# Tap weights on eight partitions and first rows of x through another queue, at the start of a convolution and feed-forward kernel

## The chip, the cores and the metric

The kernel runs on one core of one Trainium2 chip. The metric is the device time of one execution in microseconds (us). Seven kinds of work go on side by side: TensorE (PE in the profile, with its weight loads as PEld), VectorE (DVE), ScalarE (ACT), GpSimd (POOL), SyncE (SP), and the DMA engines, 16 of them, that move data for the queues of SP, ACT and POOL.

## The reference

A causal convolution of seven taps, whose weights are a softmax of a small table of 8 heads x 7 taps, and a feed-forward part on its result, with the product of two projections between:

```python
w = softmax(weight, axis=-1)                    # [8, 7]
x_pad = concat([zeros(B, 6, D), x], axis=1)     # x is [8, 3904, 192]
out[b, s, h] = sum_k w[h, k] * x_pad[b, s + k, h]   # 24 channels a head
t = out.reshape(B * S, D)                       # 31232 tokens of 192
result = (((t @ w1) * (t @ w2)) @ w3) @ w_out   # w1, w2: 192 x 1024
```

## The kernel before

**Two streams.** The 31232 tokens are cut in two halves (r = 0, 1, NS = 2), of 15616 each, and 64 partitions (Q) belong to each half. The 192 channels are three blocks of 64 (NP). So a transposed tile xT[k] holds 64 channels of both halves, and every weight tile wd[i] (i = 0 for w1, 1 for w2) is held twice: once in partitions 0 to 63 and once in 64 to 127.

**The convolution as a matmul.** A window has 64 rows of x, on the partitions, and gives 58 rows of result (ST = 64 - 6). For each head a band matrix of 64 x 64 holds the seven taps on its diagonals (Aband). It is built at the start: `band` (L252) multiplies shifted views of a diagonal (diag) by the taps on DVE into cprod (L254), and 28 small matmuls for each of four pairs of heads add them up in PSUM (L263). `conv` (L381) then multiplies windows of x (the tiles xb) by these bands (L398). Windows come in batches: batch 0 has six windows per half of the tokens, batch 1 four. The first window of each sequence has only 58 rows of x behind six rows of zeros, which is why batch 0's window 0 is loaded apart.

**The first product.** For each stretch of 512 tokens (a round R) and each 128 columns of w1 and w2, `first_factor` (L478) runs 12 matmuls (L486) into PSUM, ACT casts the one factor (L494) and DVE multiplies it by the other (L505) into abT. `second_product` multiplies abT by w3 @ w_out, which is worked out once. Rounds go in groups of four. The convolutions of later batches are put in between; their results go through DRAM (rows) and come back transposed (xT<-rows, L468).

**The order of the work** on each engine is written by hand: each engine runs its instructions in the order of the program text, and semaphores are added where data passes from one to another. The four pairs of PSUM banks (`banks`, `drained`) are handed round in that order too. A DMA is issued by an engine's queue in the same order as its other instructions.

**The start**, which the change touches:

- ACT's queue loads the table `weight` into wall, one partition of 56 values (L144). Then ACT loads its table of functions (L164).
- DVE clears some tiles (L157 to L163), among them window 0 of batch 0 of xb.
- SP's queue loads the first quarter of the columns of w1 and w2 as fp32 into wfirst (L171), 64 partitions.
- POOL's queue, which also casts to bf16 as it moves, loads batch 0 of x (L179, two loads), makes the two diagonals (L183), loads window 0's 58 rows of each half (L189, two loads), batch 1 (L126), and then the other quarters of the weights (L176) and further batches (L126). Between them POOL casts one half of wfirst into wd (`cast_w`, L193) and copies weights from the lower to the upper partitions (`copy_w`, L197).
- TensorE runs six matmuls on zeros (`warm`, L213), which give nothing and only occupy it.
- The softmax: greatest value, subtraction (DVE, L223, L224), exponential (ACT, L226), sum, reciprocal, product (DVE, L228 to L230), all on one partition. Two matmuls with a row of zeros and ones (half) spread the result to 128 partitions (L237), DVE copies it (L239), and two more matmuls on zeros follow.
- Then the four bands (`put` moves them, L584), three weight casts on ACT, the two halves of batch 0's convolution (moved by `move_all`, whose copies stand in `move`, L581), three transposes on TensorE (L456), batch 1's convolution, and the first parts of the first product.

Of the kernel before, what the change touches and what calls it, by code (L numbers as in the profile page):

```python
# [16 lines left out]
def kernel(  # L17
# [10 lines left out]
    nc = tc.nc  # L28

    B, S, D = x.shape  # L30
    H, K = weight.shape
# [3 lines left out]
    PAD = K - 1  # L35

    NS = 2
    TS = B * S // NS
# [4 lines left out]
    Q = 64  # L43
    ST = Q - PAD
# [22 lines left out]
    const = ctx.enter_context(tc.tile_pool(name="const", bufs=1))  # L67
# [10 lines left out]
    def banks():  # L78
        p = free.pop(0)
        return p, pairs[:, NS * p:NS * p + NS, :]  # L80
# [4 lines left out]
    def drained(p):  # L85
        assert p not in free
        free.append(p)
# [17 lines left out]
    x_rows = x.rearrange("b s d -> (b s) d")  # L105
    xb_of, zero_rows = {}, {}

    def x_spans(r, i, m):
        return bass.AP(tensor=x.tensor, offset=(r * TS + tok(i) - PAD) * D,
                       ap=[[D, Q], [ST * D, m], [1, D]])  # L110
# [29 lines left out]
            else:  # L140
                tiles.append((xb, 0))

    wall = const.tile([1, H, K], FP32)
    nc.scalar.dma_start(out=wall, in_=weight.rearrange("(o h) k -> o h k", o=1))  # L144

    n0 = SIZES[0] // 2
    xb0 = work.tile([128, 2 * n0, D], BF16, tag="xb", bufs=5, name="xb")
    xb_of[0] = [(xb0, 0), (xb0, n0)]
    wfirst = work.tile([Q, 2, NP, DFF // 4], FP32, tag="abT", bufs=GROUP, name="wfirst")
# [1 line left out]
    tiny = const.tile([128, 1], FP32)  # L151
    ones = const.tile([128, 1], BF16)
    zeros = const.tile([128, 128], BF16)
    half = const.tile([1, 3 * Q], BF16)
    ident = const.tile([128, 128], BF16)
    diag = const.tile([128, Q + PAD], BF16)
    nc.vector.memset(zeros, 0.0)  # L157
    nc.vector.memset(tiny, 0.0)
    nc.vector.memset(ones, 1.0)
    nc.vector.memset(xb0[:, 0, :], 0.0)  # L160
    nc.vector.memset(half, 0.0)
    nc.vector.memset(half[:, Q:2 * Q], 1.0)
    nc.vector.memset(ident, 0.0)  # L163
    nc.scalar.activation(out=tiny, in_=tiny, func=ACT.Exp)  # L164

    WC = (0, DFF // 4, DFF // 2, DFF * 3 // 4, DFF)
    wd = [const.tile([128, NP, DFF], BF16, name=f"wd{i}", tag=f"wd{i}") for i in range(2)]
    w_rows = [w.rearrange("(k q) f -> q k f", q=Q) for w in (moe_w1, moe_w2)]

    for i in range(2):  # L170
        nc.sync.dma_start(out=wfirst[:, i], in_=w_rows[i][:, :, 0:WC[1]])  # L171

    def load_w(part):
        cs = slice(WC[part], WC[part + 1])
        for i in range(2):
            nc.gpsimd.dma_start(out=wd[i][0:Q, :, cs], in_=w_rows[i][:, :, cs])  # L176

    def load_x0(r):
        nc.gpsimd.dma_start(out=xb0[Q * r:Q * r + Q, 1:, :], in_=x_spans(r, 1, 2 * n0 - 1))  # L179

    load_x0(0)
    for p0 in (0, Q):
        nc.gpsimd.affine_select(  # L183
            out=diag[p0:p0 + Q], in_=ones[p0:p0 + Q].to_broadcast([Q, Q + PAD]),
            pattern=[[-1, Q + PAD]], compare_op=ALU.is_equal, fill=0.0, base=0,
            channel_multiplier=1)
    load_x0(1)
    for r in range(NS):
        nc.gpsimd.dma_start(out=xb0[Q * r + PAD:Q * r + Q, 0, :],  # L189
                            in_=x_rows[r * TS:r * TS + ST, :])  # L190
    load_x(1)
    def cast_w(i, r, f):
        f(out=wd[i][Q * r:Q * r + Q, :, 0:WC[1]], in_=wfirst[:, i])  # L193

    def copy_w(part, i, f):
        cs = slice(WC[part], WC[part + 1])
        f(out=wd[i][Q:128, :, cs], in_=wd[i][0:Q, :, cs])  # L197

    load_w(1)
    cast_w(1, 1, nc.gpsimd.tensor_copy)  # L200
    load_w(2)
    load_x(2)
    for i in range(2):
# [6 lines left out]
    def warm(n):  # L210
        p, t = banks()
        for j in range(n):
            nc.tensor.matmul(t[:, j % 2, :], zeros, zeros[:, 0:1].to_broadcast([128, CH]),  # L213
                             start=True, stop=True)
        drained(p)

    warm(6)

    wmax = const.tile([1, H], FP32)
    wsum = const.tile([1, H], FP32)  # L220
    wrow = const.tile([1, H, K], BF16)
    wsb = const.tile([128, 2, 2, K], BF16)
    nc.vector.reduce_max(out=wmax, in_=wall, axis=AX.X)  # L223
    nc.vector.tensor_tensor(  # L224
        out=wall, in0=wall, in1=wmax.unsqueeze(2).to_broadcast([1, H, K]), op=ALU.subtract)
    nc.scalar.activation(out=wall, in_=wall, func=ACT.Exp)  # L226
    nc.vector.tensor_copy(out=ident[0:Q, 0:Q], in_=diag[0:Q, 0:Q])
    nc.vector.reduce_sum(out=wsum, in_=wall, axis=AX.X)  # L228
    nc.vector.reciprocal(out=wsum, in_=wsum)
    nc.vector.tensor_tensor(  # L230
        out=wrow, in0=wall, in1=wsum.unsqueeze(2).to_broadcast([1, H, K]), op=ALU.mult)
    nc.vector.tensor_copy(out=ident[Q:128, Q:128], in_=diag[Q:128, 0:Q])
    pw, wbc = banks()
    wbc = wbc[:, 0, 0:H * K // 2].rearrange("p (g e k) -> p g e k", g=2, e=2)
    wrow = wrow.rearrange("p (g e a) k -> p g e a k", g=2, a=2)
    for a in range(2):
        nc.tensor.matmul(wbc, half[:, Q - Q * a:Q - Q * a + 128], wrow[:, :, :, a],  # L237
                         start=(a == 0), stop=(a == 1))
    nc.vector.tensor_copy(out=wsb, in_=wbc)  # L239
    drained(pw)  # L240
    warm(2)

# [2 lines left out]
    def band_of(h, r):  # L245
        return Aband[Q * r:Q * r + Q, h // 4, (h % 4) // 2, int(h % 2 != r), :]
# [126 lines left out]
    def segments(c0, n):  # L373
        out = []
        while n:
            m = min(n, Q - c0 % Q)
            out.append((c0 // Q, c0 % Q, m))
            c0, n = c0 + m, n - m
        return out

    def conv(b, h0, nh, evict=None):  # L381
        n = SIZES[b] // 2
        if h0 == 0:
            tag, bufs = ("alone", 1) if GRID <= b else ("convo", 2)
            convo_of[b] = work.tile([128, n, NP, NS, Q], BF16, tag=tag, bufs=bufs, name="convo")
        convo = convo_of[b]
        p, cps = banks()
        wd = nh * G

        def view(ps, r):  # L390
            return cps[ps, r, 0:n * wd].rearrange("p (w g) -> p w g", g=wd)

        for j in range(nh):
            h = h0 + j
            for c in range(2):
                xb, w0 = xb_of[b][c]
                for r in range(NS):
                    nc.tensor.matmul(  # L398
                        view(slice(Q * c, Q * c + Q), r)[:, :, j * G:(j + 1) * G],
                        band_of(h, r),  # L400
                        xb[Q * r:Q * r + Q, w0:w0 + n, h * G:(h + 1) * G],
                        start=True, stop=True)
        src = cps[:, :, 0:n * wd].rearrange("p r (w g) -> p r w g", g=wd)
        o, moves = 0, []
        for k, c0, m in segments(h0 * G, wd):
            moves.append((convo[:, :, k, :, c0:c0 + m].rearrange("p w r g -> p r w g"),
                          src[:, :, :, o:o + m]))
            o += m
        if h0 + nh == H:
            del xb_of[b]  # L410
        if evict == ():
            return p, moves
        if evict == "streams":
            assert nh == H
# [163 lines left out]
    V, A, P = nc.vector.tensor_copy, nc.scalar.copy, nc.gpsimd.tensor_copy  # L578

    def move(f, pair):  # L580
        f(out=pair[0], in_=pair[1])  # L581

    def put(f, p, dst, src):
        f(out=dst, in_=src)  # L584
        drained(p)

    cast_w(0, 0, A)
    put(A, *band(0, 0))
    put(A, *band(0, 1))
    cast_w(0, 1, A)  # L590
    made = [band(1, 0), band(1, 1)]
    put(V, *made[0])
    put(V, *made[1])
    cast_w(1, 0, A)

    def move_all(p, moves, fs):
        for f, m in zip(fs, moves):
            move(f, m)
        drained(p)
# [26 lines left out]

    move_all(*conv(0, 0, 4, ()), (V, V))
    move_all(*conv(0, 4, 4, ()), (A, A))
    for k, f in enumerate((V, V, A)):
        p, *m = pe_transpose(0, k)  # L630
        move(f, m)
        drained(p)
# [51 lines left out]
    def put_rows(b, last):  # L684
# [7 lines left out]
        out=wv, in0=wv, in1=top.unsqueeze(2).to_broadcast([128, H, K]), op=ALU.subtract)  # L692
# [5 lines left out]
        out=wv, in0=wv, in1=top.unsqueeze(2).to_broadcast([128, H, K]), op=ALU.mult)  # L698
# [84 lines left out]
```

## Time and profile before

| | us |
|---|---|
| median of three runs | 517.26 |
| the three runs | 515.74, 517.26, 519.17 |
| the profiled execution | 516.65 |
| its span | 514.9 |

The span runs from the first to the last instruction in the profile; 1.75 us of the profiled execution lie around it. PEclk, the granted clock of TensorE, is 0.999 in this execution. In the profile's rows, the first number is the start in us from the beginning of the span, the second the time taken; then come the engine, the line, the operation and, after the tiles' names, how many instructions of its kind were merged in the row. In brackets stands for how long the engine had been idle before, and what ended that. ACTq, SPq and POOLq are the issuing of DMAs and the like. The chain of waits is followed back from the last instruction, each piece to what released it.

### The profile page before, as it was taken

The page shows a single profiled execution, that of the slowest core. Times are in us where ns is not written, and L with a number is a line of the kernel's source. Part 1 is how long each engine was busy: PE and PEld are TensorE (multiplying, and loading weights), DVE is VectorE, ACT ScalarE, POOL GpSimd, SP SyncE. Part 2 cuts the span into 40 slices and gives each one's busy share as a digit, 9 for nine tenths or more (in the row PEclk, how much of TensorE's full clock was granted, in tenths as well). Part 3 has the DMA queues.
Part 4 walks back from the last instruction along what each step waited for, and adds up shares of the span by engine and source line. Part 5 has one row for each costly group of instructions (what it writes and reads, how often), then busy time and mean ns, then how long its engine had stood idle before and what let it go on. Part 6 is the DMA issues. An engine that isn't in the chain of part 4 may idle for free.

```text
span 514.9 us, 13645 instructions
## 1 busy us (share of the span) xinstructions
PE 508.2 (99%) x5608; PEld 339.2 (66%) x5608; DVE 403.4 (78%) x481; ACT 350.7 (68%) x466; POOL 321.8 (63%) x447
## 2 busy tenths in 40 slices
PE   8999999999999999999999999999999999999997
PEld 4544698555894448945489454885449844598577
DVE  6788723899958999599994999949999499972970
ACT  6877645777657776577765777657776577744762
POOL 8501624289999999799984999749997491000000
PEclk9999999999999999999999999999999999999999
DMA  9998999992974983797827798288842861035004
GB/s 116 164 154 135 141 191 210 239 182 58 179 206 144 141 103 89 226 154 110 99 91 241 139 107 97 93 244 140 102 48 93 256 114 32 1 101 172 7 3 155
DMA packets 137410, 67.91 MB, mean 132 GB/s; under 512 B 98899, under 2 KB 135939, under 8 KB 137283
## 3 DMA queue, kind: packets, MB, share of 16 engines
q0 software_dynamic: 48096, 26.92, 36.6%
q1 hardware_dynamic: 89105, 40.01, 33.3%
q8 instruction: 44, 0.72, 0.6%
q14 instruction: 19, 0.16, 0.1%
q10 hardware_dynamic: 146, 0.10, 0.1%
HBM read 39.60 MB, written 36.56 MB: 148 GB/s over the span
## 4 chain that ended last, share of the span: by engine, by line
PE 95%; DMA 2%; DVE 1%; ACT 1%; POOL 1%; issue 0%; ACTq 0%
PE pairs L486 61%; PE pairs L537 31%; PE pairs L398 2%; DMA xT<-rows 1%; PE pairs L572 1%; DVE abT L505 1%; DMA xb<-in_x_dram 1%; PE pairs L611 1%; ACT asb L494 1%; DMA wall<-in_weight_dram 0%; POOL xb L189 0%; POOL xb L179 0%; POOL xb L126 0%; POOL diag L183 0%; DVE xT L624 0%
## 5 line engine op out<-in xcount | busy, mean ns | idle before, releaser
L505 DVE TENSOR_TENSOR abT<-asb,pairs 128x1024 bf16<-128x1024 bf16 (+1 forms) x245 | 297.8, 1217 | 67.4 <-ACT asb L494 51.1
L486 PE MATMUL pairs<-xT,wd 64*128 64x512 bf16 (+3 forms) x3000 | 320.0, 371 | 1.1 <-DVE abT L505 0.4
L494 ACT CAST asb<-pairs 128x1024 bf16<-128x1024 f32 (+1 forms) x245 | 247.1, 1009 | 68.7 <-PE pairs L486 68.5
L486 PEld LDWEIGHTS <-wd 64*128 64x128 bf16 x3000 | 160.8, 94 | 154.6 <-issue 3.8
L537 PE MATMUL pairs<-W_sb,abT 128*128 128x192 bf16 x1952 | 165.0, 246 | 0.0
L537 PEld LDWEIGHTS <-abT 128*128 128x128 bf16 x1952 | 159.9, 98 | 5.3 <-issue 5.1
L542 ACT COPY osb<-pairs 128x384 f32<-128x384 f32 x122 | 58.7, 481 | 83.3 <-PE pairs L537 82.5
L331 POOL TENSOR_TENSOR acc<-acc,term 128x384 f32<-128x384 f32 (+1 forms) x120 | 107.5, 896 | 9.4
L328 POOL TENSOR_TENSOR term<-xv,wv 128x384 f32<-128x384 bf16 (+1 forms) x144 | 107.9, 749 | 0.1
L317 DVE SCALAR_TENSOR_TENSOR pairs<-xv,wv,pairs 128x384 f32<-128x384 bf16 (+1 forms) x120 | 68.7, 572 | 7.2 <-ACT pairs L315 3.4
L364 POOL DMA_DIRECT2D rows<-y x6 | 3.7, 614 | 69.9 <-DVE y L320 61.1
L334 POOL TENSOR_TENSOR y<-acc,term 128x192 bf16<-128x192 f32 (+5 forms) x60 | 26.6, 470 | 1.9
L325 POOL TENSOR_TENSOR acc<-xv,wv 128x384 f32<-128x384 bf16 (+1 forms) x24 | 18.3, 764 | 10.3 <-DMA xv<-in_x_dram 10.2
L424 ACT CAST convo<-pairs 128x864 bf16<-128x864 f32 (+9 forms) x43 | 23.8, 627 | 0.1
L424 DVE CAST convo<-pairs 128x960 bf16<-128x960 f32 (+4 forms) x10 | 8.2, 857 | 17.2 <-PE pairs L398 17.2
L320 DVE SCALAR_TENSOR_TENSOR y<-xv,wv,pairs 128x192 bf16<-128x192 bf16 (+5 forms) x60 | 18.0, 351 | 1.1
L126 POOL DMA_DIRECT2D xb<-in_x_dram x20 | 13.9, 714 | 3.8 <-DMA xb<-in_x_dram 2.5
L549 POOL DMA_DIRECT2D out_dram<-osb x8 | 6.1, 764 | 14.7 <-ACT osb L542 12.0
L342 POOL DMA_DIRECT2D xb<-in_x_dram x20 | 15.1, 772 | 0.0
L447 POOL DMA_DIRECT2D rows<-convo x2 | 1.1, 544 | 20.7 <-DVE convo L420 20.7
L279 POOL DMA_DIRECT2D xv<-in_x_dram x12 | 13.0, 1086 | 0.0
L315 ACT ACTIVATE pairs<-xv,wv 128x384 f32<-128x384 bf16 (+1 forms) x24 | 12.8, 549 | 0.0
(67 smaller groups left out, 89.6 us busy)
## 6 DMA issues: line engine op xcount, KB each, us to landing
out_dram<-osb SPq DMA_DIRECT2D x52, 384.0 KB
xv<-in_x_dram POOLq DMA_DIRECT2D x10, 672.0 KB, 9.7
xb<-in_x_dram POOLq DMA_DIRECT2D x20, 216.0 KB, 7.4
rows<-y POOLq DMA_DIRECT2D x5, 768.0 KB, 5.0
out_dram<-osb POOLq DMA_DIRECT2D x8, 384.0 KB, 5.1
w3rows<-in_moe_w_dram POOLq DMA_DIRECT2D x2, 1024.0 KB, 11.2
xb<-in_x_dram POOLq DMA_DIRECT2D x8, 240.0 KB, 7.8
rows<-convo SPq DMA_DIRECT2D x6, 288.0 KB
```

What stands on the lines that cost most here:

```text
L317: f.scalar_tensor_tensor(out=flat, in0=xs(k), scalar=tap(k), in1=flat, op0=ALU.mult, op1=ALU.add)
L320: f.scalar_tensor_tensor(out=dst, in0=xv[:, 0:W, r, h * G + cs.start:h * G + cs.stop], scalar=tap(0), in1=by_row[:, :, r, cs], op0=ALU.mul ...
L325: f.tensor_tensor(out=flat, in0=xs(PAD), in1=wide(PAD), op=ALU.mult)
L328: f.tensor_tensor(out=term.rearrange("p (m g) -> p m g", g=G), in0=xs(k), in1=wide(k), op=ALU.mult)
L331: f.tensor_tensor(out=acc, in0=acc, in1=term, op=ALU.add)
L334: f.tensor_tensor(out=dst, in0=by_row[:, :, r, cs], in1=term[:, :, r, cs], op=ALU.add)
L424: f[e % len(f)](out=dst, in_=part)
L486: nc.tensor.matmul(p[:, r, e * n:e * n + n], wd[i][rs, k, ft * 128:(ft + 1) * 128], xT[k][rs, r0 + c0:r0 + c1], start=(k == 0), stop=(k == ...
L494: nc.scalar.copy(out=asb, in_=pa)
L505: nc.vector.tensor_tensor(out=dst, in0=asb, in1=pb, op=ALU.mult)
L537: nc.tensor.matmul(ops[:, (g - g0) * D:(g - g0) * D + D], ab[:, jt, r, g * 128:(g + 1) * 128], W_sb[:, jt, :], start=(jt == 0), stop=(jt = ...
L542: f(out=osb[:, g0:g0 + per, :].rearrange("p g d -> p (g d)"), in_=ops[:, 0:per * D])
```

## The change

- `weight` is loaded by SP's queue into eight partitions, seven values each (wall is [8, 7]).
- The softmax runs on eight partitions. The greatest value is taken with its sign turned and goes into the exponential as a bias, so the subtraction is gone. One instruction divides by the sum and puts each head's row on a diagonal of blocks (wrow is [8, 8, 7]).
- One matmul with ones on eight partitions spreads all 56 values to 128 partitions, and two copies of 64 partitions each take the heads that each half needs. There are five matmuls on zeros ahead of it instead of six.
- The two copies of the identity move from DVE to ACT.
- Window 0's 58 rows of each half are loaded as fp32 by SP's queue into a tile of their own (xfirst, cleared by DVE), ahead of wfirst, and ACT casts the whole tile into xb. POOL's queue no longer loads them; its second diagonal comes after the second load of batch 0.
- POOL casts the upper halves of both w1 and w2. ACT casts the lower halves in four pieces of 128 columns, of which three stand after the first two bands and the last after the convolution of batch 0.

```diff
-    wall = const.tile([1, H, K], FP32)
-    nc.scalar.dma_start(out=wall, in_=weight.rearrange("(o h) k -> o h k", o=1))
+    wall = const.tile([H, K], FP32)
+    nc.sync.dma_start(out=wall, in_=weight)
...
-    nc.vector.memset(xb0[:, 0, :], 0.0)
-    nc.vector.memset(half, 0.0)
-    nc.vector.memset(half[:, Q:2 * Q], 1.0)
+    nc.vector.memset(xfirst, 0.0)
+    nc.vector.memset(ones_h, 1.0)
...
+    for r in range(NS):
+        nc.sync.dma_start(out=xfirst[Q * r + PAD:Q * r + Q, :],
+                          in_=x_rows[r * TS:r * TS + ST, :])
     for i in range(2):
         nc.sync.dma_start(out=wfirst[:, i], in_=w_rows[i][:, :, 0:WC[1]])
...
     load_x0(0)
-    for p0 in (0, Q):
-        nc.gpsimd.affine_select(
...
+    diagonal(0)
     load_x0(1)
-    for r in range(NS):
-        nc.gpsimd.dma_start(out=xb0[Q * r + PAD:Q * r + Q, 0, :],
-                            in_=x_rows[r * TS:r * TS + ST, :])
+    diagonal(Q)
     load_x(1)
-    def cast_w(i, r, f):
-        f(out=wd[i][Q * r:Q * r + Q, :, 0:WC[1]], in_=wfirst[:, i])
+    def cast_w(i, r, f, c0=0, c1=WC[1]):
+        f(out=wd[i][Q * r:Q * r + Q, :, c0:c1], in_=wfirst[:, i, :, c0:c1])
...
     load_w(1)
-    cast_w(1, 1, nc.gpsimd.tensor_copy)
+    for i in range(2):
+        cast_w(i, 1, nc.gpsimd.tensor_copy)
     load_w(2)
...
-    warm(6)
+    warm(5)
...
-    nc.vector.reduce_max(out=wmax, in_=wall, axis=AX.X)
-    nc.vector.tensor_tensor(
-        out=wall, in0=wall, in1=wmax.unsqueeze(2).to_broadcast([1, H, K]), op=ALU.subtract)
-    nc.scalar.activation(out=wall, in_=wall, func=ACT.Exp)
-    nc.vector.tensor_copy(out=ident[0:Q, 0:Q], in_=diag[0:Q, 0:Q])
+    nc.vector.tensor_reduce(out=wmax, in_=wall, axis=AX.X, op=ALU.max, negate=True)
+    nc.scalar.activation(out=wall, in_=wall, func=ACT.Exp, bias=wmax)
+    nc.scalar.copy(out=ident[0:Q, 0:Q], in_=diag[0:Q, 0:Q])
     nc.vector.reduce_sum(out=wsum, in_=wall, axis=AX.X)
     nc.vector.reciprocal(out=wsum, in_=wsum)
-    nc.vector.tensor_tensor(
-        out=wrow, in0=wall, in1=wsum.unsqueeze(2).to_broadcast([1, H, K]), op=ALU.mult)
-    nc.vector.tensor_copy(out=ident[Q:128, Q:128], in_=diag[Q:128, 0:Q])
+    nc.vector.scalar_tensor_tensor(
+        out=wrow, in0=wall.unsqueeze(1).to_broadcast([H, H, K]), scalar=wsum,
+        in1=diag[0:H, 0:H].unsqueeze(2).to_broadcast([H, H, K]), op0=ALU.mult, op1=ALU.mult)
+    nc.scalar.copy(out=ident[Q:128, Q:128], in_=diag[Q:128, 0:Q])
+    nc.scalar.copy(out=xb0[:, 0, :], in_=xfirst)
...
+    nc.tensor.matmul(wbc, ones_h, wrow, start=True, stop=True)
     for a in range(2):
-        nc.tensor.matmul(wbc, half[:, Q - Q * a:Q - Q * a + 128], wrow[:, :, :, a],
-                         start=(a == 0), stop=(a == 1))
-    nc.vector.tensor_copy(out=wsb, in_=wbc)
+        nc.vector.tensor_copy(out=wsb[Q * a:Q * a + Q], in_=wbc[Q * a:Q * a + Q, :, :, a])
...
-    cast_w(0, 0, A)
     put(A, *band(0, 0))
     put(A, *band(0, 1))
-    cast_w(0, 1, A)
+    for i in range(2):
+        cast_w(i, 0, A, 0, 128)
+    cast_w(0, 0, A, 128)
     made = [band(1, 0), band(1, 1)]
     put(V, *made[0])
     put(V, *made[1])
-    cast_w(1, 0, A)
...
     move_all(*conv(0, 4, 4, ()), (A, A))
+    cast_w(1, 0, A, 128)
```

More of the change, by code (lines that the diff above doesn't have):

```diff
@@ L153 @@
     zeros = const.tile([128, 128], BF16)
-    half = const.tile([1, 3 * Q], BF16)
+    ones_h = const.tile([H, 128], BF16)
+    xfirst = const.tile([128, D], FP32)
     ident = const.tile([128, 128], BF16)
@@ L179, in load_x0, with diagonal @@
         nc.gpsimd.dma_start(out=xb0[Q * r:Q * r + Q, 1:, :], in_=x_spans(r, 1, 2 * n0 - 1))
-    load_x0(0)
-    for p0 in (0, Q):
+    def diagonal(p0):
         nc.gpsimd.affine_select(
@@ L186 @@
             channel_multiplier=1)
+    load_x0(0)
+    diagonal(0)
     load_x0(1)
-    for r in range(NS):
-        nc.gpsimd.dma_start(out=xb0[Q * r + PAD:Q * r + Q, 0, :],
-                            in_=x_rows[r * TS:r * TS + ST, :])
+    diagonal(Q)
     load_x(1)
-    def cast_w(i, r, f):
-        f(out=wd[i][Q * r:Q * r + Q, :, 0:WC[1]], in_=wfirst[:, i])
+    def cast_w(i, r, f, c0=0, c1=WC[1]):
+        f(out=wd[i][Q * r:Q * r + Q, :, c0:c1], in_=wfirst[:, i, :, c0:c1])
     def copy_w(part, i, f):
@@ L215, in warm @@
         drained(p)
-    warm(6)
-    wmax = const.tile([1, H], FP32)
-    wsum = const.tile([1, H], FP32)
-    wrow = const.tile([1, H, K], BF16)
+    warm(5)
+    wmax = const.tile([H, 1], FP32)
+    wsum = const.tile([H, 1], FP32)
+    wrow = const.tile([H, H, K], BF16)
     wsb = const.tile([128, 2, 2, K], BF16)
-    nc.vector.reduce_max(out=wmax, in_=wall, axis=AX.X)
-    nc.vector.tensor_tensor(
-        out=wall, in0=wall, in1=wmax.unsqueeze(2).to_broadcast([1, H, K]), op=ALU.subtract)
-    nc.scalar.activation(out=wall, in_=wall, func=ACT.Exp)
-    nc.vector.tensor_copy(out=ident[0:Q, 0:Q], in_=diag[0:Q, 0:Q])
+    nc.vector.tensor_reduce(out=wmax, in_=wall, axis=AX.X, op=ALU.max, negate=True)
+    nc.scalar.activation(out=wall, in_=wall, func=ACT.Exp, bias=wmax)
+    nc.scalar.copy(out=ident[0:Q, 0:Q], in_=diag[0:Q, 0:Q])
     nc.vector.reduce_sum(out=wsum, in_=wall, axis=AX.X)
     nc.vector.reciprocal(out=wsum, in_=wsum)
-    nc.vector.tensor_tensor(
-        out=wrow, in0=wall, in1=wsum.unsqueeze(2).to_broadcast([1, H, K]), op=ALU.mult)
-    nc.vector.tensor_copy(out=ident[Q:128, Q:128], in_=diag[Q:128, 0:Q])
+    nc.vector.scalar_tensor_tensor(
[3 more added lines that the diff above has]
+    nc.scalar.copy(out=xb0[:, 0, :], in_=xfirst)
     pw, wbc = banks()
-    wbc = wbc[:, 0, 0:H * K // 2].rearrange("p (g e k) -> p g e k", g=2, e=2)
-    wrow = wrow.rearrange("p (g e a) k -> p g e a k", g=2, a=2)
+    wbc = wbc[:, 0, 0:H * K].rearrange("p (g e a k) -> p g e a k", g=2, e=2, a=2)
+    nc.tensor.matmul(wbc, ones_h, wrow, start=True, stop=True)
     for a in range(2):
-        nc.tensor.matmul(wbc, half[:, Q - Q * a:Q - Q * a + 128], wrow[:, :, :, a],
-                         start=(a == 0), stop=(a == 1))
-    nc.vector.tensor_copy(out=wsb, in_=wbc)
+        nc.vector.tensor_copy(out=wsb[Q * a:Q * a + Q], in_=wbc[Q * a:Q * a + Q, :, :, a])
     drained(pw)
```

## The prediction

> **What bounds the kernel now.** I read the page first, then the chain of waits, then the stretches, then the first 15 us instruction by instruction.
>
> ```profile
> span 514.9 us, 13645 instructions
> ...
> PE 508.2 (99%) x5608; PEld 339.2 (66%) x5608; DVE 403.4 (78%) x481; ACT 350.7 (68%) x466; POOL 321.8 (63%) x447
> ...
> PE 95%; DMA 2%; DVE 1%; ACT 1%; POOL 1%; issue 0%; ACTq 0%
> ```
>
> TensorE carries 95% of the chain. Whether a few tenths at the start reach the end depends on idle time later. In the stretches (us, then PE's busy time) there is almost none:
>
> ```profile
> 60.00:90.00 30.00, 29.84 (x416) 27.63 (x415) 10.13 (x16) 13.89 (x32) 10.26 (x14) 1.00 1.14 198
> 90.00:515.00 425.00, 421.57 (x4444) 281.98 (x4443) 344.43 (x393) 291.85 (x372) 284.19 (x387) 1.00 0.64 126
> ```
>
> So a shift of the first product (L486) moves the end by about the same amount, and everything that the change touches lies before it. The chain of waits there:
>
> ```profile
> 0.81 1.21 DMA wall<-in_weight_dram
> ...
> 3.53 1.10 POOL xb L189 x2
> 4.63 0.59 POOL xb L126
> 5.22 4.19 DMA xb<-in_x_dram
> ...
> 9.45 0.43 PE pairs L398 x31
> 9.89 0.57 PE pairs L486 x6
> ```
>
> The last wait before the first product is the load of batch 1 of x, landing at 9.41. It was queued on POOL behind the two L189 loads. The mark to beat is the start of L486 in the timeline:
>
> ```profile
> 9.82 1.06 PE L486 MATMUL pairs<-xT,wd 64*128 64x348 bf16 x12
> ```
>
> **The softmax on eight partitions.**
>
> ```profile
> 0.81 0.52 ACTq L144 DMA_DIRECT2D wall<-in_weight_dram  x1
> 1.37 1.28 ACT L164 ACT_TABLE_LOAD   x1 [1.37 <-PEq L767]
> 2.05 0.20 DVE L223 TENSOR_REDUCE wmax<-wall 1x8 f32<-1x56 f32 x1 [0.57 <-DMA wall<-in_weight_dram]
> 2.28 0.33 DVE L224 TENSOR_TENSOR wall<-wall,wmax 1x56 f32<-1x56 f32 x1
> 2.77 0.23 ACT L226 ACTIVATE wall<-wall 1x56 f32<-1x56 f32 x1
> 4.23 2.23 DVE L254 TENSOR_TENSOR cprod<-diag,wsb 128x448 bf16<-128x448 bf16 x4
> ```
>
> The subtraction (0.33) goes into the exponential's bias; the table load no longer follows a DMA issue (0.52), so the exponential is not held by it. One copy out of PSUM becomes two, about +0.15 with overlap. The eight-partition load replaces one piece of 224 bytes by eight of 28; I take the same 1.21 (none in the trace is like it; +-0.3). Sum: L254 starts about 0.4 earlier, 3.85. Warm-up loses one of six matmuls, which stand in front of the spreading matmul and end earlier than it. The identity copies move from DVE to ACT and wait there for POOL's two diagonals; nothing else is ready on ACT then, and the second diagonal comes only 0.72 (one POOL load) later. Gain so far 0.4, if nothing else is late.
>
> **The first stretches of x.** POOL loses 1.10 of issue, so batch 1 could land at 8.3 instead of 9.41. In exchange SP issues wall and two loads of 58 rows x 768 bytes ahead of wfirst, and ACT must cast them before its next work. Here is the change's risk:
>
> ```profile
> 0.82 1.40 SPq L171 DMA_DIRECT2D wfirst<-in_moe_w_dram  x2
> 4.68 0.83 ACT L193 CAST wd<-wfirst 64x768 bf16<-64x768 f32 x1 [1.68 <-DMA wfirst<-in_moe_w_dram]
> ```
>
> wfirst's two issues took 0.70 each, starting at 0.82. With three issues of about 0.5 (the 0.52 of L144) ahead, they start near 2.3. How do 58 rows travel? The nearest row is a store on the same queue with rows of the same 768 bytes: 38 rows, L359. Its issue, and the DMA engines (40 slices of 277.45 to 277.70, tenths of 16 engines) when the earlier stores had drained:
>
> ```profile
> 275.37 1.31 SPq L359 DMA_DIRECT2D rows<-convo  x1
> ```
> ```profile
> DMA  0400003000003000030007300003000070000303
> ...
> q1 hardware_dynamic: 13, 0.01, 11.2%
> ```
>
> 11.2% of 16 is 1.8 engines: single packets, one after the other, on two engines. 13 packets in 0.25 us on two engines are 38 ns each. [...] I take it that each xfirst load puts 29 packets on the same two engines, 58 in all, and that wfirst's share there (192 rows over 16 engines, 12 per load) queues behind: 82. [...]
>
> The speed depends on what else these engines carry. The queues in the stretch 4 to 5 us, with POOL's loads running:
>
> ```profile
> q1 hardware_dynamic: 167, 0.16, 67.3%
> q0 software_dynamic: 162, 0.06, 51.0%
> ```
>
> 167 packets over 16 engines in 1 us: an engine gave SP's queue one per 96 ns, half of its 49 ns slots. After the change POOL's loads run from about 3 us as before, so I take 96, with 38 (alone) as the low end and 122 (two slots in five, an estimate) as the high one. The first packets of this queue came about 1.3 after its first issue:
>
> ```profile
> q1 hardware_dynamic: 9, 0.01, 10.1%
> ```
>
> (that is the stretch 2.0 to 2.5; only wall's lay before). xfirst is issued from about 1.35, so packets run from 2.6. xfirst: 2.6 + 58 x 0.096 = 8.2. wfirst: 2.6 + 82 x 0.096 = 10.5; the 0.4 us before POOL's loads start go faster (-0.6), the last receipt adds some 0.5: 10.4.
>
> **Who waits.** ACT works in order. The rows:
>
> ```profile
> 5.54 0.27 ACT L584 CAST Aband<-pairs 128x128 bf16<-128x128 f32 x1
> ...
> 6.28 1.69 ACT L193 CAST wd<-wfirst 64x768 bf16<-64x768 f32 x2
> ...
> 7.00 0.59 PE L398 MATMUL pairs<-xb,Aband 64*64 64x72 bf16 x32
> ...
> 7.18 0.82 POOL L193 CAST wd<-wfirst 64x768 bf16<-64x768 f32 x1
> ...
> 7.87 0.69 ACT L581 CAST convo<-pairs 128x192 bf16<-128x192 f32 x2
> ...
> 9.02 0.45 ACT L581 COPY xT<-pairs 128x348 bf16<-128x348 bf16 x1 [0.46 <-PE pairs L456]
> ```
>
> Behind ACT's cast of xfirst stand the two copies of Aband, then the weight casts, the eviction of the first convolution, the last weight cast, the copy of xT. From 768 elements at 0.83 and 128 at 0.27, an element costs 0.875 ns: the cast of 192 takes 0.33, a half weight cast of 384 takes 0.49. xfirst at 8.2 gives Aband at 8.2 + 0.33 + 0.54 = 9.1 and the first convolution (7.00 before) at about 9.1. Then ACT waits for the second wfirst load, 10.4: cast of wd1 0.49, rest of wd0 0.49, eviction 0.69, rest of wd1 0.49, xT 0.45 = 2.61, so the first product starts at 13.0. Against 9.82 that is +3.2. The gain of 0.4 in the softmax and of 1.1 for batch 1 lie under this wait and are worth nothing. At 38 ns wfirst is there at 2.6 + 3.1 + 0.5 = 6.2 and ACT is not held; at 122 ns it comes at 12.5 and the loss is 5.3.
>
> POOL casts both halves now (one more, 0.82, for the 1.10 saved) and waits for the same load: 10.4 to 12.0. Behind it stand two weight loads, batch 2 of x, and the copies of L197, which in before started when their load had landed:
>
> ```profile
> 2.81 0.72 POOL L179 DMA_DIRECT2D xb<-in_x_dram  x1
> ...
> 7.95 1.26 POOL L176 DMA_DIRECT2D wd<-in_moe_w_dram  x2
> 9.21 1.40 POOL L126 DMA_DIRECT2D xb<-in_x_dram  x2
> 10.80 1.59 POOL L197 COPY wd<-wd 64x768 bf16<-64x768 bf16 x2 [0.20 <-DMA wd<-in_moe_w_dram]
> ```
>
> ```profile
> 12.55 4.91 PE L486 MATMUL pairs<-xT,wd 64*128 64x164 bf16 x60 [0.24 <-DVE xT L624]
> ```
>
> In before POOL's casts ended at 8.0 and the copies at 12.4; the columns that they fill are first read after the 24 matmuls of 164 columns that head the last row, near 13.3: 0.9 to spare. Now the casts end at 12.0, the loads behind them take 1.26 and 1.40 of issue, and the copies end near 16.3, while TensorE comes to these columns at 13.3 + 3.2 = 16.5. Nothing is added, but the cover is thin: 0.5 more on POOL would cost 0.3.
>
> **The sum.** 516.65 (the profiled execution: span 514.9 and 1.75 around it) + 3.2 = 519.8. The median of the runs shown, 517.26, stands 0.6 above that execution, and its runs spread from 515.74 to 519.17; I keep the sum.
>
> **Rivals.** *It is quick enough* (faster than before). The two loads share their engines at the 38 ns end, or are spread wider. For it: they start before POOL's traffic. Then the Aband copies end near 5.9, three half casts bring ACT to 7.4, eviction 8.1, cast 8.6, xT 9.05; the first product starts near 9.4, 0.4 early, up to 0.9 if ACT's order yields more. 516.2. It decides if wfirst has landed by about 7.0, that is 50 ns per packet; against it stands the 96.
>
> *TensorE falls back to its slow start.* The row of warm-up matmuls and one from later:
>
> ```profile
> 1.07 2.74 PE L213 MATMUL pairs<-zeros 128*128 128x512 bf16 x6 [1.07 <-DVE ones L159]
> ```
> ```profile
> 68.11 2.75 PE pairs L537 x32
> ```
>
> 0.457 us for 512 columns first, later 0.086 for 192, that is 0.229 for 512: half speed at first, although the granted clock reads 1.00 in all stretches. With two pauses of 2 to 3 us each in the start, the first parts could run at half speed again; another 3.4 us or so of that costs 1.7 at most: 521.5. [...]
>
> *POOL's queue crowds SP's out* (122 ns): +5.3, 522.0.
>
> **How the numbers follow.** Main case 0.55 (its own range 518.2 to 521.0), quick 0.28 (515.7 to 516.6), slow start 0.10, crowded 0.07. Leaving out about a tenth at each end gives 515.8 to 521.4. This kernel's measurement tells about 1% (5.2 us) from no change: faster by that 0.01, slower (above 521.8, most of the crowded case and a tail of the slow start) 0.08, within 0.91.
>
> **What would show it.** In the changed profile: the cast of xfirst on ACT should idle until about 8 on its DMA, the cast of wd1 until about 10.4, and the first L486 product start near 13.0; a stretch of the DMA with few engines on SP's queue should be seen late. If ACT's Aband copies start before 6 and the first product before 9.5, the two-engine price was wrong. If the first product is 3 late but the end is not, later slack swallowed it, and the reading of the stretches was wrong.

## The result, and the profile after

The changed kernel is slower by 0.41%: 518.8 us in the median of 22 runs (517.8 to 520.47) against 516.74 (515.57 to 520.62, 22 runs). The ratio is 1.0041, with a 95% interval from 1.0028 to 1.0053, that is 1.4 to 2.7 us, 2.1 in the middle. The forecast was 519.8, 3.2 above the execution that it started from.

The page of the changed kernel, whose profiled execution took 517.8, its fastest (that of before, 516.65, lay near the middle of its own):

```profile
span 516.1 us, 13646 instructions
...
PE 509.3 (99%) x5606; PEld 338.6 (66%) x5606; DVE 402.9 (78%) x478; ACT 350.8 (68%) x470; POOL 321.1 (62%) x446
...
PE 97%; DMA 1%; DVE 1%; ACT 0%; issue 0%; POOL 0%; POOLq 0%; ACTq 0%; DVEq 0%
```

The shares hardly differ; the start does. From its timeline (line numbers after the change are two to three higher):

```profile
0.82 0.40 SPq L144 DMA_DIRECT2D wall<-in_weight_dram  x1
1.28 0.60 SPq L171 DMA_DIRECT2D xfirst<-in_x_dram  x2
1.92 1.36 SPq L174 DMA_DIRECT2D wfirst<-in_moe_w_dram  x2
...
4.17 2.23 DVE L256 TENSOR_TENSOR cprod<-diag,wsb 128x448 bf16<-128x448 bf16 x4
...
5.33 0.35 ACT L236 CAST xb<-xfirst 128x192 bf16<-128x192 f32 x1 [1.55 <-DMA xfirst<-in_x_dram]
...
6.81 0.24 PE L400 MATMUL pairs<-xb,Aband 64*64 64x72 bf16 x1
6.85 0.51 ACT L196 CAST wd<-wfirst 64x384 bf16<-64x384 f32 x1 [0.56 <-DMA wfirst<-in_moe_w_dram]
...
7.91 0.92 ACT L196 CAST wd<-wfirst 64x384 bf16<-64x384 f32 x2 [0.55 <-DMA wfirst<-in_moe_w_dram]
...
8.13 0.69 PE L400 MATMUL pairs<-xb,Aband 64*64 64x72 bf16 x31 [1.08 <-DMA xb<-in_x_dram]
...
10.95 1.92 PE L488 MATMUL pairs<-xT,wd 64*128 64x348 bf16 x12
```

Three things are to be seen. The rows of window 0 were cast at 5.33 and the last of wfirst was there at 7.91, much earlier than the forecast's 8.2 and 10.4. The wait that decided is on another transfer: the first convolution begins at 6.81, where it began at 7.00 before, stops after one matmul and goes on at 8.13, when a load of xb lands. And the first product then starts at 10.95 (9.82 before) and its first 12 matmuls take 1.92 (1.06 before). The chain of waits names the transfer, and shows what is left at the middle of the kernel:

```profile
2.46 5.63 DMA xb<-in_x_dram
...
61.08 5.39 PE pairs L574 x64
```

It is the second load of batch 0 by POOL's queue (issued at 2.46), landing at 8.09. The same load landed 3.9 after an issue at 2.81 before, at 6.7. And the matmuls themselves, grouped by shape (the two numbers behind the bar are the busy time in us and the mean ns of one), in the first 16 us, before and then after:

```profile
L486 PE MATMUL pairs<-xT,wd 64*128 64x348 bf16 x24 | 2.1, 309 | 0.0
L456 PE MATMUL pairs<-ident,convo 128*128 128x128 bf16 x9 | 0.8, 219 | 0.6 <-DVE convo L581 0.5
```
```profile
L488 PE MATMUL pairs<-xT,wd 64*128 64x348 bf16 x24 | 3.0, 399 | 0.0
L458 PE MATMUL pairs<-ident,convo 128*128 128x128 bf16 x9 | 1.2, 306 | 0.5 <-DVE convo L583 0.5
```

The same instructions run longer. So the loss has two parts: +1.13 at the first product (10.95 - 9.82), and +0.61 from there to the products for W_sb: these start at 61.08, and in the chain of before at

```profile
59.34 5.39 PE pairs L572 x64
```

which makes +1.74. Later the kernel before loses some of this lead: in it the transposed rows of the next round came late (4 matmuls at 89.16, the rest from 89.92), and after the change they did not (from 90.89 on without a pause). That leaves +1.40, which stays to the last copy (511.65 and 513.05); the spans end 1.2 apart. In the medians it is 2.1; one profiled execution cannot say which part grows in the others.

### The profile page after: what moved, and what is told of

Its sections match the earlier page's. It is cut to its first block, busy times and chain, and to the rows that moved or that the text cites. A ratio compares the mean times of both kernels' runs of the same rounds, so it can differ in the third digit from the quotient of the medians.

```text
span 516.1 us, 13646 instructions
## 1 busy us (share of the span) xinstructions
PE 509.3 (99%) x5606; PEld 338.6 (66%) x5606; DVE 402.9 (78%) x478; ACT 350.8 (68%) x470; POOL 321.1 (62%) x446
## 4 chain that ended last, share of the span: by engine, by line
PE 97%; DMA 1%; DVE 1%; ACT 0%; issue 0%; POOL 0%; POOLq 0%; ACTq 0%; DVEq 0%
PE pairs L488 61%; PE pairs L539 32%; PE pairs L400 2%; DMA xb<-in_x_dram 1%; PE pairs L574 1%; DVE abT L507 1%; PE pairs L613 1%; ACT asb L496 0%; PE pairs L458 0%; POOL xb L182 0%; DVE convo L583 0%; ACT osb L544 0%; POOL diag L185 0%; POOLq L185 0%; ACTq L544 0%
## 5 line engine op out<-in xcount | busy, mean ns | idle before, releaser
L126 POOL DMA_DIRECT2D xb<-in_x_dram x20 | 13.9, 714 | 3.9 <-DMA xb<-in_x_dram 2.7
L551 POOL DMA_DIRECT2D out_dram<-osb x8 | 6.1, 763 | 13.9 <-ACT osb L544 10.9
L400 PE MATMUL pairs<-xb,Aband 64*64 64x216 bf16 (+6 forms) x416 | 12.7, 245 | 1.1 <-DMA xb<-in_x_dram 1.1
```

Source lines behind the costliest of these rows:

```text
L400: nc.tensor.matmul(view(slice(Q * c, Q * c + Q), r)[:, :, j * G:(j + 1) * G], band_of(h, r), xb[Q * r:Q * r + Q, w0:w0 + n, h * G:(h + 1) ...
```

## The experiments

All ratios are to the kernel before, with 95% intervals. First the parts, alone and left out, and the way of the rows on SP's queue.

**x_only**: before, with the rows of window 0 alone taken over.

```diff
+    for r in range(NS):
+        nc.sync.dma_start(out=xfirst[Q * r + PAD:Q * r + Q, :], in_=x_rows[...])
     for i in range(2):
         nc.sync.dma_start(out=wfirst[:, i], ...)
...
-    for r in range(NS):
-        nc.gpsimd.dma_start(out=xb0[Q * r + PAD:Q * r + Q, 0, :], ...)
...
+    nc.scalar.copy(out=xb0[:, 0, :], in_=xfirst)
     cast_w(0, 0, A)
     put(A, *band(0, 0))
```

> The kernel before with one part of the change: window 0's rows as fp32 on SP's queue ahead of wfirst, ScalarE's cast of them ahead of its first weight cast; softmax, spreading and weight casts as before. If the rows' way is the cause (either reading of it), the second load of batch 0 lands near 8, the first product starts at 10.7 or later and the time is 1.2 to 2.5 us above before. If the loss came from the softmax or the regrouped casts, the first product starts at 9.8 +- 0.3 and the time is within 0.6 of before.

1.0059 (1.0046 to 1.0071): this part alone costs what the whole change costs, or more, 3.0 us where 1.2 to 2.5 were expected. Here ACT's whole weight cast stands ahead of the copies of Aband and waits for wfirst:

```profile
6.95 0.83 ACT L194 CAST wd<-wfirst 64x768 bf16<-64x768 f32 x1 [1.31 <-DMA wfirst<-in_moe_w_dram]
...
7.99 0.67 PE L399 MATMUL pairs<-xb,Aband 64*64 64x72 bf16 x32 [0.90 <-ACT Aband L585]
```

The first product started at 11.44. The cause of the convolution's wait is not the one expected; the place is.

**no_x**: the changed kernel, rows of window 0 back on POOL's queue.

```diff
-    for r in range(NS):
-        nc.sync.dma_start(out=xfirst[...], ...)
...
     diagonal(Q)
+    for r in range(NS):
+        nc.gpsimd.dma_start(out=xb0[Q * r + PAD:Q * r + Q, 0, :], ...)
     load_x(1)
...
-    nc.scalar.copy(out=xb0[:, 0, :], in_=xfirst)
```

> The changed kernel with window 0's rows back on POOL's queue, casting on the way; softmax and weight casts as changed. If the rows' way is the cause, the first convolution starts at 6.9 to 7.1, the first product at 9.4 to 9.8 and the time is 0 to 0.6 us below before. If the softmax or the casts are to blame, the first product stays after 10.5 and the time 1.5 or more above before.

1.0050 (1.0035 to 1.0065), so the theory fell in the form that it had: without the rows on SP's queue the loss stays. The convolution waited for x again, this time for window 0's rows on POOL's queue (issued at 3.46, the first of them landing at 7.61),

```profile
7.75 0.76 PE L398 MATMUL pairs<-xb,Aband 64*64 64x72 bf16 x32 [0.69 <-DMA xb<-in_x_dram]
```

and the first product came at 10.64. Each part alone is enough, and together they don't add up: the first convolution waits in all three kernels, but each time something else comes last, ACT's copies of Aband behind wfirst (x_only), window 0's rows (no_x) or batch 0's second load (the change).

**split** and **w_ahead**: the changed kernel with each load of 58 rows cut in two, and with wfirst's loads ahead of them.

```diff
     for r in range(NS):
-        nc.sync.dma_start(out=xfirst[Q * r + PAD:Q * r + Q, :], ...)
+        for s0, s1 in ((0, 48), (48, ST)):
+            nc.sync.dma_start(out=xfirst[Q * r + PAD + s0:Q * r + PAD + s1, :], ...)
```

> The changed kernel, each load of 58 rows cut into 48 and 10 rows. Two-engine reading: spread over more engines, the rows no longer hold two engines up, the second load of batch 0 lands by 7.2, the first product starts by 10.0 and the time is within 0.7 us of before. Order reading (wfirst, issued 1.1 us later, now runs against batch 0's loads): two more issues push wfirst a further 0.5 back, the load lands at 8 or later, the first product starts at 10.9 or later and the time stays 2 us above before.

```diff
-    for r in range(NS): ... xfirst
     for i in range(2): ... wfirst
+    for r in range(NS): ... xfirst
```

> The changed kernel with wfirst's two loads ahead of window 0's on SP's queue. Order reading: wfirst lands by 5.3 as before, batch 0's second load by 7.2, the rows of window 0 by about 6, the first product starts at 9.6 to 10.1 and the time is within 0.7 us of before. Two-engine reading: the two engines still have 58 rows more than the others, batch 0's second load lands near 8, the first product starts at 10.7 or later and the time stays 1.5 to 2.5 above before.

1.0081 (1.0068 to 1.0094) and 1.0071 (1.0059 to 1.0084). With the loads cut in two, batch 0 was in earlier, at 7.36 instead of 8.13 (no run shows how many engines the 48 and 10 rows went over), but two more issues push the second wfirst load to 3.56, and now ACT waits for that until 8.84:

```profile
7.36 0.45 PE L401 MATMUL pairs<-xb,Aband 64*64 64x72 bf16 x31 [0.48 <-DMA xb<-in_x_dram]
...
8.84 0.92 ACT L197 CAST wd<-wfirst 64x384 bf16<-64x384 f32 x2 [1.17 <-DMA wfirst<-in_moe_w_dram]
```

With wfirst ahead it is the rows that come last of all:

```profile
9.24 0.35 ACT L236 CAST xb<-xfirst 128x192 bf16<-128x192 f32 x1 [5.44 <-DMA xfirst<-in_x_dram]
```

Neither reading was right. In each of the three orders tried on SP's queue, something that stands late in it, or that it holds up, comes too late for the convolution or the first product. Next, what no_x had kept: the table's load ahead of wfirst, the softmax's form, and the speed of TensorE.

**wall_sp**: before, with one word changed.

```diff
-    nc.scalar.dma_start(out=wall, in_=weight.rearrange("(o h) k -> o h k", o=1))
+    nc.sync.dma_start(out=wall, in_=weight.rearrange("(o h) k -> o h k", o=1))
```

> The kernel before with one word changed: the table of taps is loaded by SP's queue, ahead of wfirst, instead of ACT's. Reading A (what is queued ahead of wfirst on SP makes it collide with batch 0's loads): wfirst starts 0.4 to 0.5 us later, the first convolution starts at 7.5 or later instead of 7.0, the first product at 10.4 or later with its 348-column matmuls near 400 ns, and the time is 1.2 to 2.5 us above before. Reading B (the loss without window 0's rows comes from the softmax's form or the casts): the first convolution at 7.0 +- 0.2, the first product at 9.8 +- 0.3, the time within 0.6 of before.

1.0053 (1.0034 to 1.0072). One load of 224 bytes, issued by SP ahead of wfirst, gives a loss as large as the whole change:

```profile
7.66 0.52 PE L398 MATMUL pairs<-xb,Aband 64*64 64x72 bf16 x32 [0.73 <-DMA xb<-in_x_dram]
...
10.43 1.72 PE L486 MATMUL pairs<-xT,wd 64*128 64x348 bf16 x12
```

Here too window 0's rows on POOL's queue come last: their two loads landed a median of 3.8 us after issue, where before took 3.1. wfirst was issued at 1.24 instead of 0.82, and the packets that SP's queue had moved by 3.0 us fell from 80 before to 22:

```profile
q1 hardware_dynamic: 80, 0.08, 14.8%
```
```profile
q1 hardware_dynamic: 22, 0.02, 4.1%
```

In soft_act below, which does not wait for x, there were 104; in no_x 29, and in the changed kernel 41, none of them of wfirst, whose first packet came at 3.8.

**wall_act**: the changed kernel with the table on ACT's queue. **soft_act**: before, with the softmax, the spreading matmul, the identity copies, POOL's order of the diagonals and the five matmuls on zeros taken over from the change, and the table in eight partitions but still on ACT's queue.

```diff
# wall_act, to the changed kernel
-    nc.sync.dma_start(out=wall, in_=weight)
+    nc.scalar.dma_start(out=wall, in_=weight)
# soft_act, to the kernel before
-    wall = const.tile([1, H, K], FP32)
-    nc.scalar.dma_start(out=wall, in_=weight.rearrange("(o h) k -> o h k", o=1))
+    wall = const.tile([H, K], FP32)
+    nc.scalar.dma_start(out=wall, in_=weight)
...
-    warm(6)
+    warm(5)
...
+    nc.vector.tensor_reduce(out=wmax, in_=wall, axis=AX.X, op=ALU.max, negate=True)
+    nc.scalar.activation(out=wall, in_=wall, func=ACT.Exp, bias=wmax)
...
+    nc.tensor.matmul(wbc, ones_h, wrow, start=True, stop=True)
```

> The changed kernel with the table of taps loaded by ACT's queue, so that window 0's rows and wfirst are issued 0.4 us earlier on SP's. Reading A: batch 0's second load lands 0.3 to 0.8 earlier than in the changed kernel (8.1 there), the first product starts at 10.2 to 10.7, and the time falls by 0.3 to 1.2 us. If the rows on two engines set it alone, the load stays at 7.9 or later and the time within 0.4 of the changed kernel's.

> The kernel before with the new softmax on eight partitions, the one spreading matmul and the identity copies on ACT, but the table loaded by ACT's queue as before, and window 0's rows and the weight casts as before. Reading A: wfirst has its old place, so the first convolution starts at 6.8 to 7.2, the first product at 9.5 to 9.9 and the time is within 0.6 of before. Reading B: first product after 10.3, time 1.2 or more above before.

wall_act: 1.0053 (1.0037 to 1.0070), the convolution at 8.00, the first product at 10.84. But the loads behind the table were not issued earlier, as had been expected:

```profile
1.02 0.22 DVE L161 MEMSET xfirst<- 128x192 f32 x1
1.26 0.68 SPq L171 DMA_DIRECT2D xfirst<-in_x_dram  x2
1.99 1.37 SPq L174 DMA_DIRECT2D wfirst<-in_moe_w_dram  x2
```

SP stood idle for 0.7 us ahead of them, which the profile puts down to DVE, and began when DVE had cleared xfirst (at 1.24); wfirst went at 1.99 instead of 1.92. So with the rows on SP the table's queue makes no difference to wfirst, and this run does not test what an earlier wfirst would give. soft_act: 1.0027 (1.0005 to 1.0048); its convolution started at 7.27 without a wait for x, close to what reading A said, and yet the time was not that of before. At the first product it was 0.30 behind, at the products for W_sb 1.56. Most of that is in the speed:

```profile
L485 PE MATMUL pairs<-xT,wd 64*128 64x348 bf16 x24 | 3.5, 452 | 0.0
L455 PE MATMUL pairs<-ident,convo 128*128 128x128 bf16 x9 | 1.2, 305 | 0.3 <-DVE convo L580 0.3
```

**soft_warm**, **warm_more** and **warm5** change only the matmuls on zeros, which compute nothing of the result: soft_act with more of them, the changed kernel with four in the wait for x, and before with one fewer.

```diff
# soft_warm
-    warm(5)
+    warm(7)
...
-    warm(2)
+    warm(3)
# warm_more
     put(V, *made[1])
+    warm(4)
# warm5
-    warm(6)
+    warm(5)
```

> The kernel with the new softmax alone (table loaded by ACT's queue) with seven and three matmuls on zeros instead of five and two, so that TensorE has no gap before the bands. Clock reading: transposes about 220 ns and 348-column matmuls about 310 instead of 305 and 452, first product at 9.9 to 10.3, time 0.6 to 1.6 us below the run without them, so within 0.5 of before. If speed has no part: 300 and 450 ns and the same time, 1.4 above before.

> The changed kernel with four more matmuls on zeros between the last band and the first convolution, where TensorE waits for batch 0's load. Clock reading (the wait costs twice, because TensorE is at half speed after it): the transposes take about 220 ns instead of 306 and the 348-column matmuls about 310 instead of 399, the first product starts at 10.6 to 11.0 as in the changed kernel, and the time falls by 0.5 to 1.2 us. If speed has no part, the matmuls keep 300 and 400 ns and the time stays within 0.4 of the changed kernel's.

> The kernel before with five instead of six matmuls on zeros ahead of the softmax's spreading, nothing else. Clock reading (TensorE reaches full speed only if it has no gap in its first 6 us): a gap of about 0.4 us opens before 3.75, the transposes take about 300 ns instead of 219, the 348-column matmuls 380 to 450 instead of 309, and the time is 0.5 to 1.5 us above before, though no transfer is later. If a matmul on zeros is worth nothing: the same durations as before and a time within 0.3 us.

soft_warm: 1.0018 (1.0000 to 1.0036). Its matmuls, by shape:

```profile
L485 PE MATMUL pairs<-xT,wd 64*128 64x348 bf16 x24 | 2.1, 309 | 0.0
L455 PE MATMUL pairs<-ident,convo 128*128 128x128 bf16 x9 | 1.0, 223 | 0.3 <-DVE convo L580 0.3
```

The speed came back. From the first product to the products for W_sb it took 49.53 (59.47 - 9.94) instead of 50.78 (60.90 - 10.12) in soft_act: 1.25 us from speed alone, between two profiles whose transfers were alike (104 and 102 packets on SP's queue from 2 to 3 us). The ratios to before, 1.0018 and 1.0027, go the same way, but their intervals overlap.

warm_more: 1.0047 (1.0027 to 1.0067). The durations are back (309 and 221 ns), the gain in time is not shown: in the profiled execution batch 0's load landed later still,

```profile
9.14 0.45 PE L400 MATMUL pairs<-xb,Aband 64*64 64x72 bf16 x31 [1.16 <-DMA xb<-in_x_dram]
```

and its 11 runs spread from 516.73 to 521.86. Up to 6.79, where the added matmuls begin, this kernel does the same as the changed one, and yet batch 0's load landed at 9.10 instead of 8.09 and the rows of window 0 were cast at 5.85 instead of 5.33: the same load came 1.01 us later in the one execution than in the other. At full speed it reached the products for W_sb at 61.03, level with the changed kernel (61.08) though its first product had started at 11.50 instead of 10.95: 49.53 instead of 50.13, so 0.60 saved on that stretch.

warm5: 1.0012 (0.9994 to 1.0030), no difference that can be told, and in its profile TensorE was at full speed (309 and 220 ns) with a gap of 0.36 in front of the spreading matmul. So "any gap" is too strong. Its 12 runs fall into two groups, six at 515.58 to 516.28 and five at 517.7 to 518.02, with one at 520.02; that one start in two is caught at half speed would fit, but no run profiled a start of the second group, the runs of the kernel before beside them also reach from 515.59 to 518.6, and it stays open.

**w_behind**: the changed kernel with wfirst held back until batch 0 has landed.

```diff
-    for i in range(2): ... wfirst
...
     load_x0(1)
+    gate = const.tile([128, 2], BF16)
+    nc.sync.dma_start(out=gate[Q:Q + 1], in_=xb0[Q:Q + 1, 1, 0:2])
+    for i in range(2): ... wfirst
```

> The changed kernel with wfirst's two loads held on SP's queue until batch 0's second load has landed (a two-value copy that reads it stands ahead of them). Contention reading (wfirst's rows hold batch 0's load up): that load lands by 6.5 instead of 8.1, the first convolution starts at 6.6 to 7.1; wfirst lands near 9 and the first product starts at 10.0 to 11.0. If POOL's load is slow by itself or held up by window 0's rows on their engines: it still lands after 7.5.

1.0111 (1.0094 to 1.0127). The convolution didn't wait for x, and wfirst came far too late, at 11.18 where about 9 was expected:

```profile
6.31 0.72 SPq L192 DMA_DIRECT2D gate<-xb  x1
6.82 0.89 PE L402 MATMUL pairs<-xb,Aband 64*64 64x72 bf16 x32
...
11.18 1.03 ACT L198 CAST wd<-wfirst 64x384 bf16<-64x384 f32 x2 [4.88 <-DMA wfirst<-in_moe_w_dram]
```

The gate could go at 6.31, so batch 0 had landed by then instead of at 8.09, with the rows of window 0 still ahead of everything on SP. So it is wfirst's rows that hold batch 0 up. This run also shows those 58-row loads by themselves on SP's queue, in the stretch 3 to 3.5 us:

```profile
q0 software_dynamic: 93, 0.04, 85.4%
q1 hardware_dynamic: 31, 0.02, 13.9%
```

13.9% of 16 is 2.2 engines, and 31 packets in 0.5 us on two are 32 ns each, with POOL's loads running beside.

**cast_ahead**: before, POOL's weight cast ahead of its next loads, as a try at the wait for batch 1.

```diff
-    load_w(1)
     cast_w(1, 1, nc.gpsimd.tensor_copy)
+    load_w(1)
```

> The kernel before with POOL's cast of the weights ahead of its next two weight loads (L176) instead of behind them. Contention reading: batch 1's load, which the first product waits for at 9.41, then shares the DMA engines with fewer weight rows and lands 0.3 to 0.8 earlier, the first product starts at 9.0 to 9.5 instead of 9.8 and the time is 0.2 to 0.8 us below before. If batch 1's load is set by its own rows and those ahead of it, it lands at 9.3 to 9.5 as before and the time is within 0.2.

The first product started half a microsecond earlier, and nothing waits for batch 1 any more:

```profile
9.30 1.06 PE L486 MATMUL pairs<-xT,wd 64*128 64x348 bf16 x12
```

In time it is 0.9996 (0.9977 to 1.0015): a gain of this size is below what these runs can tell. No kernel tried is shown to be faster than the one before. The starts beside each other (us; the third column is the mean ns of a 348-column matmul; each row is one profiled execution, that of w_behind the slowest of its four, those of x_only, wall_sp and soft_warm the fastest of theirs, and the ratio is of all runs):

| kernel | first product | ns | products for W_sb | ratio |
|---|---|---|---|---|
| before | 9.82 | 309 | 59.34 | 1 |
| changed | 10.95 | 399 | 61.08 | 1.0041 |
| x_only | 11.44 | 400 | 61.68 | 1.0059 |
| no_x | 10.64 | 435 | 61.27 | 1.0050 |
| wall_sp | 10.43 | 378 | 60.39 | 1.0053 |
| soft_act | 10.12 | 452 | 60.90 | 1.0027 |
| soft_warm | 9.94 | 309 | 59.47 | 1.0018 |
| w_behind | 14.26 | 438 | 64.91 | 1.0111 |

## Why the prediction was right, and where it was not

Right: the change is slower, because loads on SP's queue and POOL's loads get in each other's way (batch 0's second load landed at 8.09, but by 6.31 where wfirst was held back, in w_behind) and a wait of 1.08 opens ahead of the first product, which covers the gains; and 518.8 lies in the range. The range says little, as it also held the time of before. At the first product the forecast had +3.2, and it was +1.13; that the sum came nearer at the end is luck, as the points below show. Of its own signs against the two-engine price one came (ACT's first copy of Aband at 5.58, before 6) and one did not (the first product at 10.95, not before 9.5).

- *Two engines for 58 rows*: right in the share, 2.2 engines in w_behind. That both loads lie on the same two, 58 packets on each, and that 24 of wfirst queue behind them there, was the author's estimate from a store of 38 rows; no run shows it. What the changed kernel showed is when the packets ended: those of the rows at 4.58, those of wfirst at 7.54.
- *96 ns a packet there*: the term that was mis-sized. It was 32 ns in the stretch of w_behind, and 42 over all of the rows in the changed kernel (58 on an engine, if two share the 116, from 2.17 to 4.58), both near the low end of 38. The rate was read from a stretch in which both queues were at work (67.3% and 51.0% of 16 engines), and taken over to rows that take the time of two. The issues were shorter than taken too: wfirst's began at 1.92, not 2.3. The 0.5 put behind the last packet was read from no row, and no run shows it; here the last packet of wfirst ended at 7.54, 0.37 ahead of the cast that waited for it. So the rows were cast at 5.33, not 8.2, and the last wfirst load was there at 7.91, not 10.4. Only with wfirst ahead of them were the rows about as late as forecast: cast at 9.24 in w_ahead.
- *Who waits*: the step that failed. The forecast had ACT waiting for wfirst, and looked at the loads that the change moved. The transfer that came last was one that the change doesn't touch, batch 0's second load on POOL's queue, at 8.09 instead of 6.7. It was slowed by wfirst, which ran beside it: before had brought in 80 packets of wfirst by 3.0 us, when POOL's began, and w_behind, with wfirst held back, had the load in by 6.31. Hence also the wrong list of which parts do harm: the table's load on SP was priced at some 0.5 of issue ahead of the rows and +-0.3 of its own, and wall_sp shows that it costs 0.53% by itself, by way of POOL's loads.
- *The softmax gains 0.4*: it gained 0.06 (4.17 against 4.23). The exponential was free earlier, as forecast (2.36 against 2.77), but the table landed 0.12 later, and the product with the diagonal and the two copies took 0.27 and 0.38 where before took 0.20 and 0.19.
- *The quick case*, 0.28: it decided on wfirst landing by 7.0. That came at 7.9, and even so it would not have held, because of the load that it left out.
- *The slow start of TensorE*, set beside the main case at 0.10: it was part of what happened. The stretch behind the first product took 0.61 longer, and 1.25 was seen between soft_act and soft_warm, inside the 1.7 allowed. It should have been a term of the main case: behind the wait of 1.08 at this place the first 348-column matmuls took 399 ns instead of 309. The forecast's sum came near because a term too large in one place stood for one left out in another. The records of the granted clock that lie in the traces show when full speed began: at 5.67 before, at 12.99 after the change. In the 3.41 us up to 5.67 TensorE of before was never idle; after the change, counting back from 12.99 in steps of 3.41 (the length of half speed in wall_sp, below), it was idle for 1.57 us from 6.16 to 9.57, 1.08 of it the wait for batch 0, and for 0.30 in the step before. How much idle time is too much for the rise stays open: with 0.36 it came in warm5, with 0.24 it did not in w_ahead. Full speed was also lost again once it was there. In wall_sp (the columns are the stretch, then PE's busy time; the 0.50 ahead of the last two numbers is the granted clock):

```profile
4.98:8.39 3.41, 2.12 (x144) 1.59 (x144) 2.27 (x6) 2.94 (x6) 3.37 (x6) 1.00 1.22 136
8.39:11.81 3.42, 3.02 (x51) 2.03 (x53) 1.84 (x5) 1.79 (x5) 2.66 (x5) 0.50 1.05 126
11.81:15.22 3.41, 3.39 (x54) 2.24 (x52) 2.38 (x5) 2.25 (x4) 3.41 (x6) 1.00 1.18 141
```

The forecast took the pause's own length, 2 to 3 us, for what counts; here half speed came after one of 0.73 and some shorter ones, 1.29 idle and 2.12 busy in 3.41. No row of before shows the length of half speed that the forecast priced, 3.4; in wall_sp, x_only and split it lasted 3.41. What decides it, the runs do not show.
- *All of a shift reaches the end*: mostly. +1.74 at the products for W_sb was +1.40 at the last copy and +1.2 at the end of the span, because the kernel before loses 0.3 of its lead at a wait for transposed rows near 89.9, in a stretch where the forecast had read almost no idle time.

## What to carry to other kernels

When several queues load at once at the start, price the transfer that the next engine needs last, whoever issues it, and not only those that the edit moves: 0.4 us more ahead of a large load on one queue made loads on another take 0.7 us longer (wall_sp). A part that costs something in a stretch where everything is late may cost as much alone (x_only 1.0059 and no_x 1.0050, where the whole change had 1.0041), so leave parts out and put them in singly; here the two losses did not add up. And a wait of TensorE in its first microseconds can cost more than its length, because the work behind it may run slower: after the 1.08 of the change the 348-column matmuls took 399 ns instead of 309.

## What the runs showed of the hardware that had not been expected

- 58-row loads of 768-byte rows took the time of 2.2 engines and moved 31 rows in 0.5 us beside POOL's traffic, 32 ns a row on each of two (w_behind, 3 to 3.5 us). While it loaded wfirst, beside POOL's traffic too, SP's queue moved 167 packets in 1 us, 96 ns each if 16 engines share them (before, 4 to 5 us).
- A 224-byte load ahead of wfirst on SP's queue moved the first convolution from 7.00 to 7.66 and cost 0.53% (wall_sp).
- The granted clock reads 1.00 in stretches in which the same matmuls take 309 ns in one kernel and 452 in another (before and soft_act). The trace's records of it begin with the first rise to full speed (5.67 in before, 13.78 in soft_act); ahead of that the mean duration by shape shows the speed, and the granted clock does not. Later falls it does show (0.50 in wall_sp from 8.39 to 11.81).
- Half speed lasted 3.41 us in wall_sp, x_only (10.49 to 13.91) and split (11.17 to 14.58), and twice that in w_behind (10.83 to 17.66). In the 3.41 us ahead of it TensorE had been idle for 1.29, 2.01, 1.92 and 2.81 us. With 1.15 idle (split, 4.34 to 7.76) and 1.14 (warm_more, 8.61 to 12.02) it kept full speed.
